# A recurrence and mixture-of-experts kernel: two-block numerator loads, separate natural K and Q, and late Squares without a tie

## The chip, the cores and the metric

The kernel runs on one core of one Trainium2 chip. The metric is the device time of one execution in microseconds, the median of several. Its engines here are TensorE (PE), VectorE (DVE), ScalarE (ACT), GpSimd (POOL) and SyncE (SP), which issues most DMAs.

## The reference

A complex diagonal recurrence with an attention-like read-out (B=4, H=8, S=768, D=48), and behind it a top-1 mixture of experts over the 3072 tokens of width 384:

```python
mag = np.sqrt(a_re * a_re + a_im * a_im)
scale = np.minimum(mag, 0.999) / (mag + 1e-06)
a_re_n, a_im_n = (a_re * scale, a_im * scale)
for t in range(S):
    ar, ai = (a_re_n[:, :, t, :, None], a_im_n[:, :, t, :, None])
    new_re = ar * S_re - ai * S_im
    new_im = ar * S_im + ai * S_re
    kv = np.einsum('bhd,bhe->bhde', k[:, :, t], v[:, :, t])
    S_re, S_im = (new_re + kv, new_im)
    y[:, :, t] = np.einsum('bhd,bhde->bhe', q[:, :, t], S_re)
...
do_compute = x @ w_skip > 0
e_idx = np.argmax(xc @ w_gate, axis=1)
h = np.maximum(xc[mask] @ w1[e], 0.0)
y[mask] = gate_w[mask, None] * (h @ w2[e])
out[do_compute] = xc + y
```

Here x is y with the heads side by side, xc its rows with do_compute, E = 8 experts, F = 1024, and gate_w the chosen expert's softmax weight.

## The kernel before, in words

**Chain and blocks.** The sequence is cut into six chunks c of 128 positions, and pairs of chunks into three groups g. Each chunk is walked from its middle to both ends, so that 64 steps serve 2 sides of 2 chunks for all 32 batch-heads at once (128 partitions). The 64 steps of a group are eight blocks of 8 positions, 24 blocks i in all. For a block, `gate` turns the decay (tile `ain`, four DMAs, L233) into a normalised one: ACT squares (Square, `sq`, L264), DVE adds (L269), ACT takes Ln and Exp (L270, L271, tile `t`), DVE combines (L273), ACT takes Exp (L274), DVE multiplies `ain` by `t` (L360), and ACT writes a negated part (L364). `chain` then runs the running product, two DVE instructions a step (X at L414, W at L423); it waits for nothing but `ain`. `consume` turns the products into weights: ACT squares W (`ws`, L483), PE sums pairs (`sw`, L497), ACT takes Ln and Exp (L505, L506), DVE forms the inverse (L508, L510, L513), and then the numerator rows times W (`nw`, L488, one half K and one half Q) and the denominator rows times inverse (`iw`, L516). PE transposes both (`tp`, L631) and ACT copies them to `qk` (L638). POOL also spills the natural rows to DRAM (`kq`, L544).

**Loads of rows.** `load_qk` loads the tiles `num` (K on the left side, Q on the right) and `inv` (the reverse) for each block: four DMAs each, two a side, from SP.

**Units.** A unit (c,b) is one chunk of one batch. `unit_at` computes the scores pa on PE (L701) and masks them on DVE (`at`, L724); `unit` scales the state (RX, L739), sums it on PE (ps, L750/L751), lets ACT copy it (`st`, L753), adds K·V (ps, L760, from the natural K), lets ACT copy the new state (`T`, L767), multiplies out py (L771, L774), and makes the router logits and rows (yT L778, px L786, lg L797, xa L801), which go out by a DMA (L808). Natural K comes back from `kq` in the tile `nat`: `nat` (L555/L558) is called two units ahead. For the middle group the transposed K and Q are not held: its units' `nat` holds K and Q together (768 KB, L555) and PE transposes both (`tu`, L570). The first two units of that group get theirs in another way: `ahead` loads most of their rows early into `pre` tiles (POOL, L582), `turn_ahead` transposes them (`ta`, L594) and `straight` adds the rest (`ts`, L610).

**Order.** A class `Order` plays a virtual clock while the program is emitted: it picks steps by priority and due time and so fixes in which order instructions reach each engine's in-order queue; the scheduler of the framework refines it by its own model. `issue_after(x)` keeps an instruction from being placed ahead of x. The Square of a gate is held by two such ties, to the last Exp of the gate before (`exp_ins`) and to the last Exp of a consume (`wx_ins`).

After the last unit come the routes, and then the experts one after another (`moe`: tokens L1117 to L1161, ph L1193, hh and hl L1195/L1196, po L1225 to L1227).

Of the kernel before, what the change touches and what calls it, by code (L numbers as in the profile page):

```python
# [20 lines left out]
DM = H * D  # L21
# [92 lines left out]
class Kern:  # L114
# [133 lines left out]
    def load_qk(self, i, name):  # L248
        g, p = divmod(i, NP)
        t = self.ld.tile([128, LP, D], F32, name=f"{name}_{i}", tag=name)  # L250
        left, right = (self.k3, self.q3) if name == "num" else (self.q3, self.k3)
        self.load(g, t, left, 0, p * LP, LP, 0)
        self.load(g, t, right, 1, p * LP, LP, 0)
        return t

    def scale(self, i, n, ain):


        V, A, o = self.nc.vector, self.nc.scalar, self.order
# [8 lines left out]
        with self.tc.issue_after(self.cins) if self.cpos else ExitStack():  # L268
            V.tensor_tensor(u, sq[:, 0], sq[:, 1], ALU.add)  # L269
        A.activation(l, u, AF.Ln, bias=self.tinym)  # L270
        self.t_ins = A.activation(t, l, AF.Exp, scale=-0.5, bias=self.lnw, accum_out=self.acc[:, 1, i:i + 1]).ins  # L271
        yield o.wait(vt(N), o.act(2 * N, 3, o.t + vt(N)))
# [273 lines left out]

    def nat(self, c, b):

        if c == NCH - 1:
            return  # L550
# [3 lines left out]
        if self.spilled(g) and (c, b) not in self.near:  # L554
            self.nc.sync.dma_start(t.rearrange("p h q d -> p (h q) d"),  # L555
                                   self.kq[g][r:r + H].rearrange("h q s d -> s (h q) d"))
        else:
            self.nc.sync.dma_start(t[:, :, 0], self.kq[g][r:r + H, 0].rearrange("h s d -> s h d"))  # L558

    def turn(self, c, b):  # L560

        nc = self.nc
        t = self.nats[c, b]
        qk = self.un.tile([96, H, 4, HC], F32, name=f"qkT_{c}_{b}", tag="qkT")
        for hh in range(2):
            hs = slice(hh * 4, hh * 4 + 4)
            for q in range(2):
                tp = self.ps_tp.tile([96, 4, 2, HC], F32, name=f"tu_{c}_{b}_{hh}_{q}", tag="tp")
                for h in range(4):
                    nc.tensor.transpose(tp[:, h].rearrange("p k t -> p (k t)"), t[:, hh * 4 + h, q], self.ident)  # L570
                o = qk[:, hs, 2 * q:2 * q + 2]
                nc.scalar.copy(o[:, :, :, ::-1] if q else o, tp)
# [3 lines left out]
    def ahead(self, g):  # L576

        nc, n = self.nc, C - 2 * ENDS
        for b in range(NEAR):
            self.pre[b] = self.un.tile([C, H, 2, 2 * D], F32, name=f"pre_{b}", tag="nat")  # L580
            self.near[2 * g, b] = self.un.tile([96, H, 4, HC], F32, name=f"qkT_{2 * g}_{b}", tag="qkT")
            nc.gpsimd.dma_start(self.pre[b][0:n].rearrange("p h q d -> p (h q) d"),  # L582
                                self.kq[g][b * H:b * H + H, :, ENDS:C - ENDS].rearrange("h q s d -> s (h q) d"))

    def turn_ahead(self, c, b):
# [124 lines left out]
    def unit(self, c, b):  # L710
# [44 lines left out]
        if c < NCH - 1:  # L755
            kt = self.nats.pop((c, b))[:, :, 0]
            if ps is None:
# [40 lines left out]
        if c == NCH - 1:  # L798
            hi = self.parts[0][:, b]
            A.copy(hi.rearrange("p (a k) -> p a k", k=2 * D), px[:, :, 0:2 * D])  # L800
# [31 lines left out]
    def rows(self, c):  # L832
# [3 lines left out]
        if c == NCH - 1:  # L836
            self.lg = self.rt.tile([128, B, E + 1], F32, name=f"lg_{c}", tag="lg5")
            self.parts = [self.un.tile([128, B, DM], F32R, name=f"xa{k}", tag="nat") for k in "hl"]
        elif c % 2 == 0:
# [3 lines left out]
    def units(self, g):  # L843
        self.nat(2 * g, 0)
        self.nat(2 * g, 1)
        self.unit_at(2 * g, 0)
# [122 lines left out]
    def route1(self, b):  # L969
# [27 lines left out]
        pt = self.order.pe(200)  # L997
        hi, lo = [t[:, b] for t in self.parts]
        V.tensor_tensor(lo, self.xa[c][:, b, 0:DM], hi, ALU.subtract)
# [51 lines left out]
    def attention(self):  # L1051
        with ExitStack() as ctx:
# [15 lines left out]
            self.pr_ins, self.py_ins, self.T2, self.ain, self.QK, self.Ew, self.T, self.pa, self.W, self.ready, self.nats, self.kqt = [{} for _ in range(12)]  # L1068
            self.F_done = self.cpos = self.gates_done = self.cons_done = self.routes_done = self.units_done = self.v_done = 0
# [60 lines left out]
    def tokens(self, e, xg, xp, pt_, ph_):  # L1130
# [22 lines left out]
        for i, (b, x) in enumerate(((0, self.py_ins[2]), (1, px), (2, px), (-1, pr[3]), (3, pr[3]))):  # L1153
            with self.tc.issue_after(x):
                for k, pt in enumerate(pts):
# [292 lines left out]
```

## Time and profile before

| | us |
|---|---|
| median of 3 runs | 504.09 (503.89 to 505.27) |
| the profiled execution's own time | 504.79 |
| its span in the profile | 503.1 |
| PE busy / DVE busy / ACT busy in the span | 421.0 / 401.8 / 303.2 |
| POOL busy | 99.5 |

The profiled execution is one of its own, 0.70 us above the median. The clock granted to TensorE was 0.902 of full on the mean. Shares of busy time are averages over a first part and a second part with different limits, so the stages are read one by one below. An idle time is printed in brackets with the instruction that ended it.

### The profile page before, as it was taken

How to read it: one execution, taken by the hardware profiler on the slowest of the kernel's cores; microseconds unless marked ns; L12 is line 12 of the kernel's file. 1: busy time of each engine (PE TensorE's matmuls, PEld its weight loads, DVE VectorE, ACT ScalarE, POOL GpSimd, SP SyncE). 2: the span in 40 equal slices, each digit the busy share in tenths (PEclk: the TensorE clock that was granted, in tenths of full speed). 3: DMA queues.
4: the chain of work that ended last, by engine and by line, in shares of the span. 5: the costliest groups of instructions: out<-in, count | busy, mean ns of one | idle time of the engine just before them, and what ended most of it. 6: DMA issues, size and time to landing. Idle time of an engine off the chain costs nothing. (4 is left out here: it accounts for less than half of the span.)

```text
span 503.1 us, 10049 instructions
## 1 busy us (share of the span) xinstructions
PE 421.0 (84%) x3294; PEld 369.7 (73%) x3294; DVE 401.8 (80%) x1009; ACT 303.2 (60%) x702; POOL 99.5 (20%) x171
## 2 busy tenths in 40 slices
PE   0355654499998678889999999998999999999992
PEld 0143432389786567778878889997999999999992
DVE  4999999998989979998897967878788766866630
ACT  5868698656466687568879763332656553755420
POOL 4011111110212412072000020343301211121011
PEclk9966666579999865999999999999999999999997
DMA  4556877688977986587765529775798667865301
GB/s 97 117 120 161 203 169 177 159 205 216 262 177 198 217 207 162 129 205 185 168 173 119 124 56 273 201 208 156 228 295 264 201 203 246 246 195 182 106 23 27
DMA packets 141953, 88.83 MB, mean 177 GB/s; under 512 B 112347, under 2 KB 135372, under 8 KB 141895
## 3 DMA queue, kind: packets, MB, share of 16 engines
q1 hardware_dynamic: 135031, 71.30, 55.3%
q0 software_dynamic: 6224, 16.63, 11.6%
q8 instruction: 28, 0.46, 0.4%
q10 hardware_dynamic: 640, 0.20, 0.2%
q14 instruction: 30, 0.25, 0.2%
HBM read 63.39 MB, written 26.58 MB: 179 GB/s over the span
## 5 line engine op out<-in xcount | busy, mean ns | idle before, releaser
L414 DVE TENSOR_TENSOR X<-W,ain 128x192 f32<-128x192 f32 x192 | 67.7, 353 | 5.6 <-ACT ain L364 2.3
L1118 DVE TENSOR_TENSOR l<-r,h 128x768 fp32r<-128x768 f32 (+1 forms) x53 | 56.6, 1074 | 12.6 <-ACT h L1117 12.5
L497 PE MATMUL sw<-ws,ident 128*128 128x384 f32 x84 | 43.7, 657 | 20.5 <-ACT ws L483 20.3
L1195 ACT ACTIVATE hh<-ph 128x240 fp32r<-128x240 f32 x64 | 23.8, 374 | 52.8 <-PE ph L1193 52.8
L1117 ACT CAST h<-r 128x768 fp32r<-128x768 f32 (+1 forms) x53 | 49.2, 934 | 9.4 <-DMA r<-in_moe_w_dram 9.3
L631 PE MATMUL tp<-ident,iw 128*96 128x128 f32 x128 | 24.7, 347 | 33.1 <-DVE iw L516 29.3
L423 DVE TENSOR_TENSOR W<-X 128x96 f32<-128x96 f32 x192 | 48.7, 254 | 3.5
L1193 PE MATMUL ph<-xh,l 128*128 128x240 f32 x192 | 51.2, 275 | 0.0
L1193 PE MATMUL ph<-xh,h 128*128 128x240 f32 x192 | 49.9, 275 | 0.0
L1193 PE MATMUL ph<-xl,h 128*128 128x240 f32 x192 | 49.5, 276 | 0.2 <-DVE xl L1147 0.2
L631 PEld LDWEIGHTS tp<-ident,iw 128*96 128x96 f32 x128 | 18.8, 162 | 36.4 <-ACT t L271 19.6
L638 ACT COPY qk<-tp 96x256 f32<-96x256 f32 x128 | 39.6, 370 | 6.7 <-PE tp L631 6.3
L1225 PE MATMUL po<-h,hh 128*120 128x384 f32 x128 | 43.4, 339 | 0.0
L497 PEld LDWEIGHTS sw<-ws,ident 128*128 128x128 f32 x84 | 19.2, 250 | 32.6 <-ACT ws L483 22.6
L1226 PE MATMUL po<-l,hh 128*120 128x384 f32 x128 | 42.9, 337 | 0.0
L1227 PE MATMUL po<-h,hl 128*120 128x384 f32 x128 | 41.1, 343 | 0.0
L771 PE MATMUL py<-at,vt 128*64 128x128 f32 x384 | 40.2, 280 | 0.0
L880 POOL DMA_INDIRECT xs<-xa,sl x24 | 28.3, 1180 | 42.5 <-DVE sl L953 22.1
L1193 PEld LDWEIGHTS ph<-xh,l 128*128 128x128 f32 x192 | 36.4, 189 | 0.0
L1196 DVE SCALAR_TENSOR_TENSOR hl<-ph,hh 128x240 fp32r<-128x240 f32 x64 | 25.7, 403 | 13.1 <-ACT hh L1195 13.0
L724 DVE TENSOR_TENSOR at<-pa,mask 128x512 f32<-128x512 f32 x48 | 32.6, 684 | 4.3 <-PE pa L701 4.2
L1193 PEld LDWEIGHTS ph<-xh,h 128*128 128x128 f32 x192 | 35.6, 189 | 0.3 <-issue 0.2
(254 smaller groups left out, 1078.1 us busy)
## 6 DMA issues: line engine op xcount, KB each, us to landing
r<-in_moe_w_dram SPq DMA_DIRECT2D x24, 512.0 KB, 5.1
r<-in_moe_w_dram SPq DMA_DIRECT2D x32, 384.0 KB, 7.5
kq<-nw POOLq DMA_DIRECT2D x24, 192.0 KB, 3.8
kq<-iw POOLq DMA_DIRECT2D x24, 192.0 KB, 3.3
vt<-in_v_dram SPq DMA_DIRECT2D x24, 192.0 KB, 3.4
out_dram<-xa SPq DMA_DIRECT2D x24, 192.0 KB, 2.8
nat<-kq SPq DMA_DIRECT2D x6, 768.0 KB
ain<-in_a_im_dram SPq DMA_DIRECT2D x90, 48.0 KB, 2.7
```

The lines of the kernel that those rows point to most:

```text
L414: V.tensor_tensor(X, prev.unsqueeze(1).to_broadcast([128, 2, 2, D]), windows(ain[:, :, j]), ALU.mult)
L423: self.cins = V.tensor_tensor(W[:, j, ::-1], X[:, :, 0], X[:, :, 1], ALU.add).ins
L497: nc.tensor.matmul(sw, self.ident, ws[:, :, c], start=(c == 0), stop=(c == 1))
L631: nc.tensor.transpose(tp[:, jj], src[:, s * 4 + jj], self.ident)
L638: nc.scalar.copy(o, tp[:, :, :, cc].rearrange("p j s b -> p b s j"))
L771: PE.matmul(py[j * 64:j * 64 + 64, hp], vt_[:, 2 * hp + j], at[:, 2 * hp + j], start=True, stop=(c == 0))
L1117: nc.scalar.copy(hi[:, ks], raw)
L1118: nc.vector.tensor_tensor(lo[:, ks], raw, hi[:, ks], ALU.subtract)
L1193: pe = PE.matmul(ph, w[:, k, js], x[:, k], start=(n == 0), stop=(n == len(terms) - 1))
L1225: PE.matmul(po, hh[:, j, sl], w2h[:, j], start=(j == 0), stop=False)
L1226: PE.matmul(po, hh[:, j, sl], w2l[:, j], start=False, stop=False)
L1227: pe = PE.matmul(po, hl[:, j, sl], w2h[:, j], start=False, stop=(j == NF - 1))
```

## The change

Four edits. (1) `load_qk`: a `num` tile holds 16 rows and is loaded every second block; block i+1 takes its half from a dictionary. `inv` stays at 8 rows. (2) Natural K lies in two tiles that live through the attention part, kn0 and kn1 (units in turn, 384 KB each, for all c under 5); natural Q lies in tiles `natq`, loaded only for the middle group's units other than the first two, at L576 of the changed kernel, two units ahead of its use in `unit_at`. The rows loaded ahead are split likewise: their K goes to kn0 and kn1, their Q to `natq` tiles, four POOL DMAs of half the size instead of two. (3) The Square of `scale` keeps its ties for i under 19 only, and that of `scale_last` loses the tie to `wx_ins`. (4) The tiles for the last chunk's rows in two parts (xah, xal) are cut in two, to fit the new tags. `SUMS` is empty, so the branch on it is never taken, and `LOADED` is not used.

```diff
+SUMS = ()
+TIED = 19
...
     def load_qk(self, i, name):
         g, p = divmod(i, NP)
-        t = self.ld.tile([128, LP, D], F32, name=f"{name}_{i}", tag=name)
-        left, right = (self.k3, self.q3) if name == "num" else (self.q3, self.k3)
-        self.load(g, t, left, 0, p * LP, LP, 0)
-        self.load(g, t, right, 1, p * LP, LP, 0)
-        return t
+        rows = LP * self.rows_at_once[name]
+        ts = self.kqs[name]
+        if i not in ts:
+            t = self.ld.tile([128, rows, D], F32, name=f"{name}_{i}", tag=name)
+            left, right = (self.k3, self.q3) if name == "num" else (self.q3, self.k3)
+            self.load(g, t, left, 0, p * LP, rows, 0)
+            self.load(g, t, right, 1, p * LP, rows, 0)
+            for k in range(rows // LP):
+                ts[i + k] = t[:, k * LP:k * LP + LP]
+        return ts.pop(i)
...
-        with self.tc.issue_after(self.exp_ins), self.tc.issue_after(self.wx_ins):
+        with self.tc.issue_after(self.exp_ins), self.tc.issue_after(self.wx_ins) if i < TIED else ExitStack():
             A.activation(sq, ain[:, 0:2], AF.Square, scale=1.0 / 0.999)
...
-        with self.tc.issue_after(self.exp_ins), self.tc.issue_after(self.wx_ins):
+        with self.tc.issue_after(self.exp_ins):
             A.activation(sq, ain[:, 0:2], AF.Square, accum_out=self.acc[:, 0, i:i + 1])
...
-    def nat(self, c, b):
+    def knat(self, n):
+        return self.kns[n % 2]
+
+    def nat(self, n, end):
+        while self.k_done <= n and self.k_done < min(end, (NCH - 1) * B):
+            self.nc.sync.dma_start(self.knat(self.k_done), self.rows_of(*divmod(self.k_done, B), 0))
+            self.k_done += 1
+
+    def natq(self, c, b):
+        if self.spilled(c // 2) and (c, b) not in self.near:
+            t = self.natqs[c, b] = self.half(f"natq_{c}_{b}")
+            self.nc.sync.dma_start(t, self.rows_of(c, b, 1))
...
-        t = self.nats[c, b] = self.un.tile([C, H, 2, 2 * D], F32, name=f"nat_{c}_{b}", tag="nat")
...
     def turn(self, c, b):
-        t = self.nats[c, b]
+        t = self.knat(c * B + b), self.natqs.pop((c, b))
...
-            self.pre[b] = self.un.tile([C, H, 2, 2 * D], F32, name=f"pre_{b}", tag="nat")
+            self.pre[b] = self.knat(2 * g * B + b), self.half(f"pre_{b}")
...
-            nc.gpsimd.dma_start(self.pre[b][0:n].rearrange("p h q d -> p (h q) d"),
-                                self.kq[g][b * H:b * H + H, :, ENDS:C - ENDS].rearrange("h q s d -> s (h q) d"))
+            for q in range(2):
+                nc.gpsimd.dma_start(self.pre[b][q][0:n], self.rows_of(2 * g, b, q, ENDS, C - ENDS))
...
+            nx = c * B + b + 2
+            if (c, b) not in self.near and nx < (c // 2 + 1) * 2 * B:
+                self.natq(*divmod(nx, B))
...
-        nx = c * B + b + 2
-        if nx < (c // 2 + 1) * 2 * B:
-            self.nat(*divmod(nx, B))
+        nx = c * B + b + 3
+        if b == 0 and c % 2 == 0:
+            self.natq(*divmod(nx, B))
+        self.nat(nx - 1, (c // 2 + 1) * 2 * B)
...
+            self.kns = [self.half(f"kn{i}", "nat") for i in range(2)]
...
+            self.kqs, self.rows_at_once = dict(num={}, inv={}), dict(num=2, inv=1)
```

Because the planner's costs and the tiles change, the order of other instructions moves too. Lines of the changed kernel are higher by 2 to 34; the names say which instruction it is. On ACT, at the block 19's gate and unit (2,0)'s state, the order before was (sq and t are block 19's, st, ps and T unit (2,0)'s, ws block 17's):

```order
L270 ACTIVATE sq_2275<-sq_2275,col 128x384
L271 ACTIVATE t_2276,acc<-sq_2275,col 128x384
L274 ACTIVATE t_2276,acc<-sq_2275 128x384
L753 COPY st_165<-ps_0_2355 96x8x48
L767 COPY T_0_2367<-ps_0_2355 96x384
L364 ACTIVATE ain_2198<-ain_2198 128x384
L483 ACTIVATE ws_2530<-W_2327 128x768
```

and in the changed kernel (qk from tp is the copy of block 16's transposed iw, the second Square, on `ain_2222`, is block 20's):

```order
L285 ACTIVATE sq_2231<-sq_2231,col 128x384
L784 COPY st_165<-ps_0_2306 96x8x48
L286 ACTIVATE t_2232,acc<-sq_2231,col 128x384
L666 COPY qk_0_2136<-tp_0_2_2458 96x32x2x4
L666 COPY qk_1_2137<-tp_0_2_2458 96x32x2x4
L666 COPY qk_0_2136<-tp_1_2_2465 96x32x2x4
L666 COPY qk_1_2137<-tp_1_2_2465 96x32x2x4
L289 ACTIVATE t_2232,acc<-sq_2231 128x384
L272 ACTIVATE sq_2675<-ain_2222 128x768
L798 COPY T_0_2318<-ps_0_2306 96x384
```

The copy st moved ahead of both Exps of block 19, the four copies of block 16's transposed iw came ahead of the second Exp, and block 20's Square, 31 rows further down before, now stands right behind it.

On SP, around the loads of natural rows for the middle group's units, before (num and inv are block 18's, nat_2 is unit (2,2)'s 768 KB, ain block 21's):

```order
L233 DMA num_2456<-in_k_dram 32x8x48 x2
L233 DMA num_2456<-in_q_dram 32x384 x2
L233 DMA inv_2522<-in_q_dram 32x8x48 x2
L233 DMA inv_2522<-in_k_dram 32x384 x2
L555 DMA nat_2_2563<-kq_119 128x16x96
L233 DMA ain_2713<-in_a_re_dram 32x8x48
L686 DMA vt_170<-in_v_dram 128x8x48
L233 DMA ain_2713<-in_a_re_dram 32x8x48
```

and in the changed kernel (kn_171 and kn_172 are kn0 and kn1, first for units (2,0) and (2,1), at the end kn0 for (2,2); ain_2222 is block 20's and ain_2666 block 21's; inv is block 18's; natq_2 and natq_3 are the Q halves of (2,2) and (2,3)):

```order
L569 DMA kn_171<-kq_119 128x8x96
L569 DMA kn_172<-kq_119 128x8x96
L236 DMA ain_2222<-in_a_re_dram 32x8x48 x2
L236 DMA ain_2222<-in_a_re_dram 32x384 x2
L236 DMA ain_2222<-in_a_im_dram 32x8x48 x2
L236 DMA ain_2222<-in_a_im_dram 32x384 x2
L576 DMA natq_2_2240<-kq_119 128x8x96
L576 DMA natq_3_2514<-kq_119 128x8x96
L236 DMA inv_2473<-in_q_dram 32x8x48 x2
L236 DMA inv_2473<-in_k_dram 32x384 x2
L236 DMA ain_2666<-in_a_re_dram 32x8x48
L569 DMA kn_171<-kq_119 128x8x96
```

Unit (2,2)'s Q half moved ahead of block 18's inv, its K half stands behind it and behind the first DMA of block 21's ain. Block 18's num has gone from here: it was loaded with two blocks together earlier.

On DVE, from block 19's gate sum to block 16's iw, before (the last row is iw of block 16; X and W are block 17's steps; sq is block 19's; oh, cnt, ohs and cand are the router's):

```order
L269 TENSOR_TENSOR sq_2275<-sq_2275 128x384
L414 TENSOR_TENSOR X_5_2425<-W_2327,ain_2041 128x192
L508 TENSOR_TENSOR ws_2303<-sw_2417,ws_2303 128x8x48
L423 TENSOR_TENSOR W_2327<-X_5_2425 128x2x48
L510 SCALAR_TENSOR_TENSOR ws_2303<-ws_2303 128x8x48
L414 TENSOR_TENSOR X_6_2440<-W_2327,ain_2041 128x192
L273 SCALAR_TENSOR_TENSOR sq_2275<-sq_2275,t_2276 128x384
L513 SCALAR_TENSOR_TENSOR inv_2218<-inv_2218,ws_2303 128x384
L423 TENSOR_TENSOR W_2327<-X_6_2440 128x2x48
L965 TENSOR_TENSOR ohs<-ohs,cnt_2503 128x8
L944 TENSOR_TENSOR cand_2395<-oh_2397,pr_2430 128x64
L516 TENSOR_TENSOR iw_2505<-inv_2218,W_2189 128x768
```

and in the changed kernel up to the same iw:

```order
L973 RECIPROCAL xa_1499<-se_2342 128x4
L957 TENSOR_TENSOR oh_2348<-oh_2348,act_2341 128x64
L976 SCALAR_TENSOR_TENSOR base_2343<-act_2341,base_2343 128x8
L523 TENSOR_TENSOR ws_2259<-sw_2368,ws_2259 128x8x48
L438 TENSOR_TENSOR W_2278<-X_3_2357 128x2x48
L997 TENSOR_REDUCE cnt_2454<-oh_2348 128x8
L525 SCALAR_TENSOR_TENSOR ws_2259<-ws_2259 128x8x48
L429 TENSOR_TENSOR X_4_2363<-W_2278,ain_2002 128x192
L528 SCALAR_TENSOR_TENSOR inv_2174<-inv_2174,ws_2259 128x384
L438 TENSOR_TENSOR W_2278<-X_4_2363 128x2x48
L284 TENSOR_TENSOR sq_2231<-sq_2231 128x384
L531 TENSOR_TENSOR iw_2456<-inv_2174,W_2145 128x768
```

iw and the ws and inv ahead of it moved up past two X steps, block 19's sum stands just ahead of iw, and block 19's second step (sq from t) comes behind it. A few rows further on, block 17's ws (L508) stands ahead of the masking at of unit (2,1) (L724); before, it stood behind it. Near 165 to 180 us two more swaps: PE has the first ta of unit (2,0) ahead of sw_14, and DVE the gate product ain_16 ahead of ws_14. Behind 198 us PE has sw_16 ahead of the transposes of nw_16.

## Rows read from the trace of the kernel before

**Rows 1.** Stages (us; us, then per engine busy (instructions); PEclk, DMA share, GB/s)
```profile
165.00:200.00 35.00, 25.60 (x154) 22.08 (x153) 31.53 (x85) 26.52 (x67) 10.20 (x19) 0.65 0.84 195
200.00:205.00 5.00, 5.00 (x27) 4.45 (x27) 4.95 (x21) 1.50 (x6) 0.08 (x1) 0.73 0.82 185
...
205.00:210.50 5.50, 3.70 (x32) 2.62 (x30) 5.50 (x26) 3.35 (x8) 0.00 (x0) 1.00 0.48 119
...
220.00:260.00 40.00, 39.37 (x339) 32.51 (x338) 33.57 (x79) 31.87 (x77) 9.32 (x12) 1.00 0.75 182
...
400.00:495.00 95.00, 93.85 (x686) 93.51 (x685) 58.54 (x97) 43.81 (x84) 15.05 (x16) 1.00 0.55 169
```

**Rows 2.** The longest waits of PE from 226 to 495 us (in all, times, longest)
```profile
PE px L786 <- ACT yT L778: 1.5, 3, 0.6
```

**Rows 3.** PE in order of time (start us, us, instruction, [idle before <-releaser])
```profile
176.04 2.91 PE L497 MATMUL sw<-ws,ident 128*128 128x384 f32 x4
...
198.74 3.78 PE L701 MATMUL pa<-qkT 96*128 96x128 f32 x16 [0.56 <-ACT qkT L616]
...
207.68 0.81 PE L751 MATMUL ps<-RX,perm 96*96 96x384 f32 x2
...
210.52 1.56 PE L760 MATMUL ps<-vt,nat 128*96 128x48 f32 x16 [1.81 <-ACT st L753]
...
213.70 1.08 PE L631 MATMUL tp<-ident,iw 128*96 128x128 f32 x8
214.61 1.46 PE L497 MATMUL sw<-ws,ident 128*128 128x384 f32 x4
...
219.64 1.05 PE L570 MATMUL tu<-ident,nat 128*96 128x128 f32 x8 [1.46 <-DMA nat<-kq]
```

**Rows 4.** ACT in order of time, same columns
```profile
199.01 0.85 ACT L483 ACTIVATE ws<-W 128x768 f32<-128x768 f32 x1
...
209.49 0.52 ACT L274 ACTIVATE t<-sq 128x384 f32<-128x384 f32 x1 [0.75 <-DVE sq L273]
...
210.01 0.46 ACT L753 COPY st<-ps 96x384 f32<-96x384 f32 x1
```

**Rows 5.** SP in order of time, and DMA issues with KB and us to landing
```profile
211.20 0.82 SPq L233 DMA_DIRECT2D inv<-in_q_dram  x2
...
213.51 0.38 SPq L555 DMA_DIRECT2D nat<-kq  x1
213.99 2.37 SPq L233 DMA_DIRECT2D ain<-in_a_re_dram  x1
...
nat<-kq SPq DMA_DIRECT2D x10, 384.0 KB, 3.9
```

**Rows 6.** DVE in order of time from 206 us
```profile
206.22 0.32 DVE L414 TENSOR_TENSOR X<-W,ain 128x192 f32<-128x192 f32 x1
...
207.54 0.55 DVE L508 TENSOR_TENSOR ws<-sw,ws 128x384 f32<-128x384 f32 x1
```

**Rows 7.** The numerator's loads: one, the tile's view, and the first user on DVE
```profile
12.00 0.91 SPq L233 DMA_DIRECT2D num<-in_q_dram  x2
...
DMA to landing us min/median/max: 2.0/3.0/4.1
...
17.82 0.95 DVE L488 TENSOR_TENSOR nw<-num,W 128x768 f32<-128x768 f32 x1
```

**Rows 8.** Waits of DVE from 222 to 300 us, same columns
```profile
DVE ain L360 <- ACT t L274: 2.5, 2, 1.5
DVE X L414 <- ACT ain L364: 2.3, 2, 1.7
```

**Rows 9.** DVE near 179 us, and POOL's loads ahead of it
```profile
177.97 0.56 DVE L273 SCALAR_TENSOR_TENSOR sq<-sq,t 128x384 f32<-128x384 f32 x1 [0.74 <-ACT t L271]
...
180.33 0.56 DVE L508 TENSOR_TENSOR ws<-sw,ws 128x384 f32<-128x384 f32 x1 [0.84 <-ACT ws L506]
...
167.26 1.84 POOL L582 DMA_DIRECT2D pre<-kq  x2 [0.54 <-issue]
```

More of the change, by code (lines that the diff above doesn't have):

```diff
@@ L41 @@
 VX = 12
+SUMS = ()
+TIED = 19
+LOADED = 1500
 NEAR, ENDS = 2, 3 * LP
@@ L267, in scale @@
         yield o.wait(0, o.act(2 * N, 1, o.t + (2500 if i else 6000)))
-        with self.tc.issue_after(self.cins) if self.cpos else ExitStack():
-            V.tensor_tensor(u, sq[:, 0], sq[:, 1], ALU.add)
-        A.activation(l, u, AF.Ln, bias=self.tinym)
+        m2, cost, done = u, vt(N), o.t + vt(N)
+        if i in SUMS:
+            m2 = self.ps_at.tile([128, n, D], F32, name=f"m2_{i}", tag="pa")
+            for c in range(2):
+                self.nc.tensor.matmul(m2, self.ident, sq[:, c], start=(c == 0), stop=(c == 1))
+            cost, done = 0.0, o.pe(2600)
+        else:
+            with self.tc.issue_after(self.cins) if self.cpos else ExitStack():
+                V.tensor_tensor(u, sq[:, 0], sq[:, 1], ALU.add)
+        A.activation(l, m2, AF.Ln, bias=self.tinym)
         self.t_ins = A.activation(t, l, AF.Exp, scale=-0.5, bias=self.lnw, accum_out=self.acc[:, 1, i:i + 1]).ins
-        yield o.wait(vt(N), o.act(2 * N, 3, o.t + vt(N)))
+        yield o.wait(cost, o.act(2 * N, 3, done))
         V.scalar_tensor_tensor(u, l, 0.0, t, ALU.max, ALU.add)
@@ L545, in keep, with half, rows_of @@
                                      src[side * 64:side * 64 + m].rearrange("p j c d -> p j (c d)"))
-    def nat(self, c, b):
-        if c == NCH - 1:
-            return
+    def knat(self, n):
[8 more added lines that the diff above has]
+            self.nc.sync.dma_start(t, self.rows_of(c, b, 1))
+    def half(self, name, tag="natq", pool=None):
+        return (pool or self.un).tile([C, H, 2 * D], F32, name=name, tag=tag)
+    def rows_of(self, c, b, q, t0=0, t1=C):
         g, cc = divmod(c, 2)
-        t = self.nats[c, b] = self.un.tile([C, H, 2, 2 * D], F32, name=f"nat_{c}_{b}", tag="nat")
         r = cc * BH + b * H
[L554 to L558, printed above, removed]
+        return self.kq[g][r:r + H, q, t0:t1].rearrange("h s d -> s h d")
     def turn(self, c, b):
         nc = self.nc
-        t = self.nats[c, b]
+        t = self.knat(c * B + b), self.natqs.pop((c, b))
         qk = self.un.tile([96, H, 4, HC], F32, name=f"qkT_{c}_{b}", tag="qkT")
@@ L755, in unit @@
         if c < NCH - 1:
-            kt = self.nats.pop((c, b))[:, :, 0]
+            kt = self.knat(c * B + b)
             if ps is None:
@@ L798, in unit @@
         if c == NCH - 1:
-            hi = self.parts[0][:, b]
+            hi = self.parts[0][b // 2][:, b % 2]
             A.copy(hi.rearrange("p (a k) -> p a k", k=2 * D), px[:, :, 0:2 * D])
@@ L837, in rows @@
             self.lg = self.rt.tile([128, B, E + 1], F32, name=f"lg_{c}", tag="lg5")
-            self.parts = [self.un.tile([128, B, DM], F32R, name=f"xa{k}", tag="nat") for k in "hl"]
+            self.parts = [[self.un.tile([128, 2, DM], F32R, name=f"xa{k}{j}", tag=t) for j in range(B // 2)]
+                          for k, t in (("h", "natq"), ("l", "nat"))]
         elif c % 2 == 0:
@@ L843, in units @@
     def units(self, g):
-        self.nat(2 * g, 0)
-        self.nat(2 * g, 1)
+        n, end = 2 * g * B, (2 * g + 2) * B
+        self.nat(n + 1, end)
+        self.natq(2 * g, 2)
         self.unit_at(2 * g, 0)
@@ L997, in route1 @@
         pt = self.order.pe(200)
-        hi, lo = [t[:, b] for t in self.parts]
+        hi, lo = [t[b // 2][:, b % 2] for t in self.parts]
         V.tensor_tensor(lo, self.xa[c][:, b, 0:DM], hi, ALU.subtract)
@@ L1067, in attention @@
             self.scat, self.pre, self.near, self.xa = [], {}, {}, {}
-            self.pr_ins, self.py_ins, self.T2, self.ain, self.QK, self.Ew, self.T, self.pa, self.W, self.ready, self.nats, self.kqt = [{} for _ in range(12)]
-            self.F_done = self.cpos = self.gates_done = self.cons_done = self.routes_done = self.units_done = self.v_done = 0
+            self.pr_ins, self.py_ins, self.T2, self.ain, self.QK, self.Ew, self.T, self.pa, self.W, self.ready, self.natqs, self.kqt = [{} for _ in range(12)]
+            self.F_done = self.cpos = self.gates_done = self.cons_done = self.routes_done = self.units_done = self.v_done = self.k_done = 0
             self.rx_t = 0.0
             self.cq, self.routes = [], []
+            self.kqs, self.rows_at_once = dict(num={}, inv={}), dict(num=2, inv=1)
             o = self.order = Order()
@@ L1160, in tokens @@
                     for n, xa in enumerate(self.parts):
-                        PE.matmul(pt, xa[:, b, ks(k)], self.ohx[b], start=(i + n == 0), stop=True, skip_group_check=True)
+                        PE.matmul(pt, xa[b // 2][:, b % 2, ks(k)], self.ohx[b], start=(i + n == 0), stop=True, skip_group_check=True)
         A.copy(xh[:, 0], pts[0])
```

4 lines of the change are left out of this document (2 added, 2 removed).

## The prediction, as it was made

> **What bounds the kernel now.** I read the table of stages first [rows 1]. Ahead of 220 us DVE carries the program: 31.53 of 35 us busy from 165 to 200, 5.50 of 5.50 from 205 to 210.5. From 220 us on PE is full: 39.37 of 40 at once, 93.85 of 95 in the last long stretch. So the end is the moment at which PE becomes full, near 219.6 us, plus a fixed pile of PE work. A change counts if it moves that moment, or opens or closes a gap in PE behind it. The gaps behind it are small: from 226 to 495 us the largest group of waits is 1.5 us in all [rows 2].
>
> The waits just ahead of that moment come next [rows 3]. PE waits 1.81 us at 210.52 for ACT's copy st (L753) before unit (2,0)'s K·V product, and 1.46 us at 219.64 for the transfer of `nat` before the transposes tu (L570) of unit (2,2). Behind them stand two causes. ACT's copy st starts at 210.01 although PE wrote its input by 208.5 (L751 at 207.68, 0.81 long): t_19's two Exps (L271, L274) stand ahead of it in ACT's order, the second after a wait of 0.75 for DVE [rows 4]. And the 768 KB of `nat` are issued only at 213.51, behind inv_18's loads, which waited for iw_16 (L516) until 211.20 [rows 5]; PE could start 6.1 us after the issue.
>
> **The change, part by part.** The sum is made against the profiled execution's own 504.79 us; the median of the three runs is 504.09, so I carry the difference over to the median. About 0.3% (1.5 us) is what a measurement here can tell from no change.
>
> *Numerator rows for two blocks.* 48 of the 96 DMAs of 48 KB go, and the other 48 double: two of them held SP 0.91 us [rows 7], so 22 us of SP's time in all, and as many bytes move as before. No engine's waits behind 20 us name `num` [rows 2, 3, 8], so this is worth 0. What covers its risk: the first load is twice as long, and its user (nw, L488) starts at 17.82 us, while the load was issued from 12.00 to 12.91 [rows 7] and a load of this kind lands 2.0 to 4.1 us after issue [rows 7], thus by 17.0 at the latest; twice the bytes cost at most a few tenths more than that. Cover 0.8 us; if it breaks, DVE loses those tenths at the start and so does the end.
>
> *Natural K and Q apart.* The bytes are the same; unit (2,2)'s Q half is issued ahead of inv_18's loads (second order fence), its K half behind them and behind the first ain_21 load, and not before unit (2,0)'s K·V product has read kn0, which ends about 212.1. A 384 KB load landed 3.9 us after issue [rows 5], against 6.1 for 768 KB. On DVE ws_16 (L508) and with it iw_16 stand ahead of five instructions more (X and W of the chain, cnt, sq_19's sum; third order fence), which from 206.22 to ws_16's start at 207.54 hold 1.3 us [rows 6], and with the W behind them some 1.5: iw_16 ends near 209.6 instead of 211.1. So inv_18's loads, which take some 2.2 us before the next issue (211.20 to 213.51 [rows 5]), end near 211.8; K is issued at 212.3, or, if the ain_21 load ahead of it takes SP the 2.37 us that one took at 213.99, at 214.3. It lands between 216.2 and 218.2. PE reaches tu, walking its new order with the durations of [rows 3], near 217.2. So of the 1.46 us between 0.5 and 1.46 go; I take 1.2, nearer the early issue, since the long ain load stood behind 768 KB just issued. The Trainium skill speaks against splitting: "DMA: Bandwidth & Descriptors", section Bandwidth, asks for transfers of 1 MiB and more, since each pays a fixed cost. The trace bears that out (6.1 us for 768 KB, 3.9 for half), and if the halves came one behind the other, 7.8 us would stand against 6.1 and the 1.2 would go.
>
> *The order near 208 to 220.* st is now ahead of t_19's Exps (first order fence), and PE has iw_16's transposes (1.08 us for eight, at 213.70 [rows 3]) ahead of the K·V product, in the gap of 1.81. They can run from 209.7 to 210.7, so the K·V product starts 0.2 later than now with 1.1 us of work less behind it: 0.9, which I take; the whole 1.81 is the upper bound, 0 the lower, if DVE's iw_16 is no earlier than it was. On the other side DVE gets ws_17 (L508) ahead of unit (2,1)'s masking `at` in its order; ws_17 needs sw_17, which by the same walk comes through ACT's Ln and Exp near 217.7, so DVE idles about 1 us there. PE waits for it only at py of (2,1) and RX of (2,1), where it is 1 to 2 us ahead, so I take 0, at worst -1.0.
>
> *The stretch 165 to 200.* ta of unit (2,0) goes ahead of sw_14, its copy ahead of sq_16's Ln, which starts some 0.4 us later (a copy such as st takes 0.46 [rows 4]); DVE waited 0.74 for that chain at 177.97 and 0.84 for ws_14 at 180.33 [rows 9]. Now ain_16 stands ahead of ws_14; by the same durations DVE waits about 1.1 and 0.8, 1.9 for 1.6. That is -0.3 on an engine that sets the end. The K half of the rows loaded ahead is the first of four smaller transfers from 167.26 on [rows 9], and its transposes run behind sw_14, which ended near 179: 11 us of cover, where a load of 768 KB landed within 6.1.
>
> *Squares no longer tied (i of 19 and up).* They free DVE of waits for ACT behind 222 us: 2.5 for t (L274) and 2.3 for ain (L364) [rows 8]. PE is full there, so this is worth 0 in the time; its use is slack for DVE, which repays the 1 us above. If PE were not full, up to 4.8 us.
>
> *The rest.* The MoE part has the same order; the split of the parts xa hi/lo changes no instruction. 0.
>
> Sum: 0.9 + 1.2 - 0.3 = 1.8 us less: 503.0 for the profiled execution, **502.3 us** against the median.
>
> **Rivals.**
> 1. *Nothing arrives* (504.1). DVE is never idle from 205 to 210.5 [rows 1]; if the 1 us of idle at ws_17 and the later RX hold PE back where it would be ahead, or K lands at 218.2 or later, both gains end as other waits. For: two engines are near their limit at once. Against: iw_16 itself moves forward on DVE.
> 2. *Slower: PE's clock comes up later.* The granted clock was 0.65 from 165 to 200, 0.73 from 200 to 205 and 1.00 after [rows 1]; sw's pair took 2.91 us at the lower level (176.04) and 1.46 at the full one (214.61) [rows 3]. It rose while PE worked without a gap behind 198.74. The new order puts sw_16 ahead of nw_16's transposes there, and sw_16 needs ACT's ws_16. If that opens a gap of a microsecond and the half clock stays until 210, the 3.70 us of work that PE did between 205 and 210.5 [rows 1] takes 3.7 more; 1.8 of that falls into the old gap, and with rival 1 the time is 504.1 + 1.9 = 506.0. It decides at sw_16: no gap, no rival. Against: ACT writes ws_16 from 199.01 to 199.86 [rows 4], while pa keeps PE busy until 202.5 [rows 3]. "TensorE: Matmul & The Clock Gate" of the Trainium skill, Part 1, says that the low clock is the default and steady work releases it; by that rule, a gap there would cost in this way, and the trace agrees (0.65 in a stretch with PE busy 25.60 of 35).
> 3. *More is won* (500.3): the 1.81 and 1.46 go whole, the -0.3 stays, and the waits behind 226 halve with the new places of the ACT copies: 504.1 - 3.3 - 0.8 + 0.3. For: those waits are for an ACT copy [rows 2].
> 4. *The change does not do what it says*: the Squares are freed, but sit in ACT's order ahead of copies that PE needs; a Square of this width takes 0.85 us (ws at 199.01 [rows 4]), four of them (sq_20 to sq_23) make at worst 3.4 us of PE gaps; half of that with nothing won gives 504.1 + 1.7 = 505.8. Against: ACT is busy only 31.87 of 40 us there [rows 1].
>
> **How the numbers follow.** The forecast, a gain of 1.0 to 2.6 us, has 0.42; rival 3 has 0.10; rival 1 has 0.28; rivals 2 and 4 have 0.11 and 0.09. The forecast's lower part (under 1.5 us) counts as no change: 0.04 of it. So faster by over 0.3% (under 502.6) 0.48, within 0.3% 0.32 (0.28 + 0.04), slower (over 505.6) 0.20. The range reaches from a little below rival 3's time, 500.0, to rival 2's, 506.0, and leaves out less than half of each, some 0.04 and 0.1. The forecast's own range is 501.5 to 503.1.
>
> **What would show it.** Right: iw_16's transposes run before the K·V product of (2,0), st copied before 209.5, tu of (2,2) starting before 218.5 with a wait under 0.5 us, PE becoming full 1.5 to 2.5 us earlier, and the stretch behind it unchanged in PE work; DVE waits at ain and X behind 222 gone without moving the end. Wrong: K landing behind 218.5, a wait for RX or `at` of (2,1) on PE of over 1 us, the clock at its lower level behind 205, ACT Squares ahead of a copy that PE waits for, or DVE later at 198 by more than 0.5 us.

## The result, and the profile after

The changed kernel takes **498.98 us** (median of 4 runs, 497.84 to 499.60); the kernel before took 504.68 on the same chip (503.89 to 506.97). The ratio is 0.9875, interval 0.9841 to 0.9909: faster by 1.2%, or 6.3 us by the ratio. The forecast was 1.8 us; the time lies below the low end of the range. The profiled execution took 499.22 us with a span of 497.5; before it was 504.79 and 503.1. So 5.6 us are to be found between the two traces.

The table of stages of the changed kernel, against [rows 1] (us; us, then per engine busy (instructions) in the order PE, PEld, DVE, ACT, POOL; PEclk, DMA share, GB/s):

```profile
165.00:200.00 35.00, 27.65 (x157) 24.16 (x157) 33.25 (x92) 25.70 (x66) 11.38 (x21) 0.64 0.81 194
...
205.00:210.50 5.50, 5.50 (x58) 4.35 (x58) 5.45 (x21) 3.96 (x12) 1.15 (x2) 1.00 0.81 194
220.00:260.00 40.00, 39.84 (x361) 32.78 (x360) 36.59 (x87) 33.62 (x85) 6.46 (x11) 1.00 0.69 174
```

DVE does 33.25 us of work from 165 to 200 where it did 31.53, and from 205 to 210.5 PE is full where it was busy 3.70 of 5.50.

To find where the 5.6 us arise I cut both programs at the same piece of work: the transposes tpe at the end of block 15, which follow directly on those of iw_15 (ts). Before they started at 197.54, after at 195.14. **2.4 us are won ahead of that point.** Behind it, the same columns, first the kernel before:

```profile
197.54:222.00 24.46, 20.39 (x158) 16.84 (x158) 24.02 (x84) 14.36 (x37) 7.14 (x9) 0.89 0.71 167
222.00:345.00 123.00, 121.90 (x1179) 104.82 (x1179) 100.31 (x274) 77.21 (x192) 26.48 (x32) 1.00 0.65 166
345.00:493.80 148.80, 147.65 (x1123) 145.51 (x1119) 101.00 (x212) 73.73 (x140) 25.70 (x28) 1.00 0.63 194
```

And the changed kernel:

```profile
195.14:222.00 26.86, 26.61 (x191) 21.01 (x191) 26.00 (x89) 16.93 (x45) 11.11 (x10) 0.87 0.84 206
222.00:345.00 123.00, 121.78 (x1218) 105.76 (x1217) 102.97 (x290) 74.96 (x188) 22.26 (x32) 1.00 0.60 159
345.00:488.30 143.30, 142.39 (x1048) 140.75 (x1048) 96.43 (x192) 71.64 (x135) 24.86 (x27) 1.00 0.62 195
```

PE is practically full from 195 us on, where it became full near 219.6 before. Its idle time up to 222 us falls from 24.46 - 20.39 = 4.07 to 0.25; from there to 345 it is 1.10 and 1.22, and up to PE's last matmul 1.15 and 0.91. Together **3.9 us less idle**. Against it stand some 0.8 us, because more of the work now falls on the lower clock (0.87 of 26.86 us, 0.89 of 24.46). 2.4 + 3.9 - 0.8 = 5.5, of 5.6.

The second part is what the prediction spoke of. PE in the changed kernel (start us, us, instruction, [idle before <-releaser]), against [rows 3]:

```profile
195.14 0.64 PE L677 MATMUL tpe<-ident,e 128*96 128x128 f32 x2
...
207.47 1.05 PE L659 MATMUL tp<-ident,iw 128*96 128x128 f32 x8
208.36 1.48 PE L791 MATMUL ps<-vt,kn 128*96 128x48 f32 x16
...
214.85 0.60 PE L598 MATMUL tu<-ident,kn 128*96 128x128 f32 x4
```

iw_16's transposes stand ahead of the K·V product, and the waits of 1.81 for st and 1.46 for `nat` are both gone. ACT's copy st and SP's loads (same columns) show why, against [rows 4, 5]:

```profile
207.01 0.45 ACT L784 COPY st<-ps 96x384 f32<-96x384 f32 x1
```

```profile
207.35 0.84 SPq L236 DMA_DIRECT2D inv<-in_q_dram  x2
...
210.02 0.40 SPq L569 DMA_DIRECT2D kn<-kq  x1
```

st is copied at 207.01, not 210.01. inv_18's loads go at 207.35, not 211.20, and unit (2,2)'s K half at 210.02, 4.8 us ahead of its transposes.

The first part, 2.4 us ahead of 197.5, the prediction did not have at all: it expected 0.3 us of loss there. DVE carries that part: up to tpe it is busy 175.8 us before and 175.6 after, and its waits from 20 us on are 8.1 us in all before and 5.7 after: the 2.4 us. Before (in all, times, longest):

```profile
DVE ws L508 <- ACT ws L506: 3.2, 5, 0.8
DVE sq L273 <- ACT t L271: 2.6, 7, 0.7
...
DVE nw L488 <- PE ts_True L610: 0.6, 1, 0.6
```

and after:

```profile
DVE ws L523 <- ACT ws L521: 3.1, 6, 0.8
DVE sq L288 <- ACT t L286: 1.1, 5, 0.3
```

From 165 us on they are 2.3 before (the 0.74 and 0.84 of [rows 9] and the 0.6 for nw) and 0.5 after. The experiments are about this part first.

### The profile page after: what moved, and what is told of

It is laid out like the page before. It is cut to its first block, busy times and chain, and to the rows that moved or that the text cites. A ratio compares the mean times of both kernels' runs of the same rounds, so it can differ in the third digit from the quotient of the medians.

```text
span 497.5 us, 10005 instructions
## 1 busy us (share of the span) xinstructions
PE 419.4 (84%) x3294; PEld 368.3 (74%) x3294; DVE 401.6 (81%) x1009; ACT 301.6 (61%) x702; POOL 99.5 (20%) x173
## 5 line engine op out<-in xcount | busy, mean ns | idle before, releaser
L1267 POOL DMA_INDIRECT out_dram<-og,idx x16 | 19.7, 1228 | 83.2 <-DVE og L1266 46.2
L914 POOL DMA_INDIRECT xs<-xa,sl x24 | 26.9, 1121 | 45.5 <-DVE sl L987 20.2
```

## The experiments

The expectations set two theories of the gain against each other, beside others. **SP's time** (Theory B): SP issues loads without a gap for long stretches, and a load that gates need is late because SP was busy with others; 48 DMAs fewer give that time back. **The order** (Theory A): the time comes from where the instructions now stand on each engine, whichever edit moved them. Every kernel's time is told as a ratio to the kernel before on the same chip, since that kernel itself took 504 to 507 us on some chips and 518 on another. The traces are of one execution each.

### One part alone

The two-block numerator loads, put into the kernel before (`load_qk` as in the change, and this line):

```diff
+ self.kqs, self.rows_at_once = dict(num={}, inv={}), dict(num=2, inv=1)
```

> Theory A (order: each part gains where it moves the order of instructions): the two-block numerator loads alone change DVE's order from block 12 on, at about 150 us, so they give the part of the gain between 150 and 198 us: 1.0 to 1.6 us less than before, nothing between 100 and 115 us. Theory B (queue: fewer DMAs on SP make every load land earlier): this part alone gives most of the 5.6 us, 3 to 5 us less. As predicted blind: 0.

Measured: 499.6 us, ratio **0.9881** (0.9826 to 0.9937). Nearly the whole gain, from the part that the sum put at 0. tpe starts at 194.97, as in the changed kernel, and DVE's waits up to it are 5.4 us. Of the two of [rows 9] 0.18 is left at sq and nothing at ws (DVE, start us, us, instruction):

```profile
176.63 0.56 DVE L278 SCALAR_TENSOR_TENSOR sq<-sq,t 128x384 f32<-128x384 f32 x1 [0.18 <-ACT t L276]
...
178.25 0.96 DVE L365 TENSOR_TENSOR ain<-ain,t 128x768 f32<-128x768 f32 x1
...
179.29 0.55 DVE L513 TENSOR_TENSOR ws<-sw,ws 128x384 f32<-128x384 f32 x1
```

The gate's product ain stands ahead of the weights ws here, so DVE has work while ACT makes them; near 158 and 168 us ws stands first. In the kernel before all three pairs stand reversed (ain 158.19, ws 159.23; ain 169.20, ws 170.44; ws 180.33, ain 180.97). With them iw_13 starts at 170.37, not 172.45, and PE's transposes of it at 171.37, not 173.46. In the kernel before ACT waited 1.42 us, until 176.26, to copy the outcome of these transposes (qkT), and block 16's Ln and Exp stood behind that copy; in num_alone it waits for DVE's sum ahead of them, 0.64 us. The changed kernel has the same three pairs as num_alone. No load need come earlier for this: ACT's Squares wait 4.6 us for DMAs from 60 to 230 us in num_alone and 4.4 before. The other 2.9 us of num_alone arise behind tpe and are not broken down here.

K and Q in tiles of their own alone (the change with `dict(num=1, inv=1)` and all Squares tied):

> Theory A: natural K and Q apart change PE's order from about 100 us on and remove the wait for nat at 219.6, so they give 0.9 us between 100 and 115 us and 1.5 to 2 us between 198 and 222: 2.0 to 3.0 us less than before. Theory B: little, under 1 us, since as many bytes and more DMAs go through SP.

Measured: 504.67 us, ratio **0.9979** (0.9945 to 1.0013): no change that shows.

The freed Squares alone:

```diff
- with self.tc.issue_after(self.exp_ins), self.tc.issue_after(self.wx_ins):
+ with self.tc.issue_after(self.exp_ins), self.tc.issue_after(self.wx_ins) if i < TIED else ExitStack():
```

> Theory A: the untied Squares change DVE's order from 222 us on only, where PE is full, so 0 to 0.9 us less than before; DVE's waits for ACT's t and ain behind 222 us, 4.8 us in all, go. Rival C (PE is not really full behind 222 us and follows DVE): 2 to 4 us less.

Measured: 509.22 us, ratio **1.0057** (1.0014 to 1.0101): slower. Two things lie in its profile. Behind 222 us rival 4 is there as described: a Square stands directly ahead of the copy st, and PE waits. ACT, then PE:

```profile
238.30 0.83 ACT L265 ACTIVATE sq<-ain 128x768 f32<-128x768 f32 x1
239.03 0.46 ACT L754 COPY st<-ps 96x384 f32<-96x384 f32 x1
```

```profile
239.54 1.56 PE L761 MATMUL ps<-vt,nat 128*96 128x48 f32 x16 [0.74 <-ACT st L754]
```

The other lies ahead of 222, where this kernel has the same order of instructions as the one before. The Square of one gate there, in this kernel and in the kernel before:

```profile
201.59 0.84 ACT L265 ACTIVATE sq<-ain 128x768 f32<-128x768 f32 x1 [3.41 <-DMA inv<-in_k_dram]
```

```profile
196.54 0.84 ACT L264 ACTIVATE sq<-ain 128x768 f32<-128x768 f32 x1 [0.27 <-DMA inv<-in_k_dram]
```

The same instruction waits 3.41 us for a DMA in one execution and 0.27 in the other. Everything behind it on ACT is late by that: the copies qkT, for which PE waits 3.71 us at 203.79 before the products pa (0.56 in [rows 3]). In 23 executions of the kernel before on that chip the time ran from 503.40 to 512.11 us; how long this wait was in them no trace shows. The row names `inv`, but what the Square reads is `ain`. SP in the kernel before shows where that load stands (start us, us, instruction):

```profile
186.06 1.01 SPq L233 DMA_DIRECT2D num<-in_k_dram  x2
187.11 1.44 SPq L233 DMA_DIRECT2D num<-in_q_dram  x2
188.65 0.86 SPq L233 DMA_DIRECT2D inv<-in_q_dram  x2
189.55 0.45 SPq L233 DMA_DIRECT2D inv<-in_k_dram  x1
190.11 1.80 SPq L233 DMA_DIRECT2D ain<-in_a_re_dram  x4
191.96 2.54 SPq L233 DMA_DIRECT2D ain<-in_a_im_dram  x4
194.53 0.42 SPq L233 DMA_DIRECT2D inv<-in_k_dram  x1
```

Each row follows the last within 0.3 us, from 179.5 on and up to 206.93, and SP's waits in that time are 3.0 us in all, so `ain` goes out when SP reaches it. A DMA of 48 KB takes 0.45 us of SP, four of `ain` 1.80; `num` takes some 2.4 us ahead of them here. The last of `ain` was issued by 194.50, the page gives `ain` 2.7 us from issue to landing, and the Square started at 196.54: no slack. In num_alone SP stands still from 202.52 to 208.83, before from 206.93 to 211.20.

In ties_alone, though, the load was not late because SP was busy with others. SP stood still from 173.16 to 178.32, by the trace for a DMA (`inv`, 5.1 us), and worked without a gap from there on:

```profile
171.11 2.05 SPq L234 DMA_DIRECT2D ain<-in_a_re_dram  x4
178.32 2.21 SPq L234 DMA_DIRECT2D ain<-in_a_im_dram  x4
...
195.76 2.04 SPq L234 DMA_DIRECT2D ain<-in_a_im_dram  x4
```

The last `ain` of that Square went out by 197.80, 3.3 us later than before. With its queue full SP did not make up for the stop. The kernel before has such a stop too, 3.9 us near 174 for `ain`, with the DMA engines busy all the while (share 1.05 to 1.16 from 172 to 178).

### Is it the number of DMAs?

The two-block tile, but filled by eight DMAs of 48 KB, as many as before. First in the kernel before:

```diff
- self.load(g, t, left, 0, p * LP, rows, 0)
+ for k in range(rows // LP):
+     self.load(g, ts[i + k], left, 0, (p + k) * LP, LP, 0)
```

(and the same for `right`; an excerpt).

> The kernel before, with the numerator's rows loaded for two blocks at once, but in eight DMAs of 48 KB instead of four of 96 KB: as many DMAs on SP as before, 96. Theory B (SP's issue time, 0.45 us for each DMA, makes the loads of ain late near 196 us): no gain, within 1.5 us of before, and ACT's Square of block 19 waits for a load. Theory A (the order that two-block loads bring): the gain of num_alone stays, 4 us or more.

Measured: 519.77 us, ratio **1.0047** (0.9998 to 1.0096), against 0.9881 with four larger DMAs. The same edit in the changed kernel:

> The changed kernel with its two-block numerator rows brought by eight DMAs of 48 KB instead of four of 96 KB, nothing else changed. Theory B (SP's issue time): the gain goes, within 0.5% of before. If the number of DMAs on SP mattered only for the kernel before, the gain of 1.2 to 1.4% stays.

Measured: 507.78 us, ratio **1.0013** (0.9979 to 1.0047), against 0.9859 for the changed kernel in another set (below). The bytes and the tiles are the same, the DMAs are twice as many, and the gain is gone in both. But the number of DMAs is not all that differs. DVE's order is back as well: the three pairs of ain and ws stand as in the kernel before. And the eight DMAs stand in one row ahead of `ain`, some 5 us of SP where four take some 2 before. In num_two_blocks_small SP, and ACT's Square that follows:

```profile
80.22 1.98 SPq L233 DMA_DIRECT2D num<-in_k_dram  x2
82.24 1.20 SPq L233 DMA_DIRECT2D num<-in_q_dram  x2
83.48 0.92 SPq L233 DMA_DIRECT2D num<-in_k_dram  x2
84.44 0.91 SPq L233 DMA_DIRECT2D num<-in_q_dram  x2
```

```profile
91.16 0.84 ACT L269 ACTIVATE sq<-ain 128x768 f32<-128x768 f32 x1 [2.49 <-DMA ain<-in_a_im_dram]
```

The kernel before has this Square at 86.00 without a wait. So here the queue does make a load late; but block 19's Square, whose wait was expected, ran at 201.33 without one. The waits of ACT's Squares for DMAs from 60 to 230 us (in all, times, longest), in the kernel before:

```profile
ACT sq L264 <- DMA num<-in_k_dram: 2.5, 1, 2.5
...
ACT sq L264 <- DMA ain<-in_a_im_dram: 1.6, 2, 1.2
...
ACT sq L264 <- DMA inv<-in_k_dram: 0.3, 1, 0.3
```

in the kernel before with the eight small DMAs:

```profile
ACT sq L269 <- DMA ain<-in_a_im_dram: 8.0, 4, 2.5
...
ACT sq L269 <- DMA inv<-in_q_dram: 4.5, 2, 3.3
```

in the changed kernel with them:

```profile
ACT sq L272 <- DMA ain<-in_a_im_dram: 10.4, 4, 5.0
...
ACT sq L272 <- DMA num<-in_k_dram: 2.5, 1, 2.5
...
ACT sq L272 <- DMA inv<-in_q_dram: 1.7, 1, 1.7
```

and in the changed kernel:

```profile
ACT sq L272 <- DMA ain<-in_a_im_dram: 3.7, 2, 2.1
```

4.4, 12.5, 14.6 and 3.7 us. tpe starts at 197.54, 201.96, 204.15 and 195.14. These waits go some way to tell the loss with the small ones, but not the gain (4.4 against 3.7). DVE's waits up to tpe tell both: 8.1, 13.2, 14.6 and 5.7 us, and tpe's start less these is 189.4, 188.8, 189.6 and 189.4. num_two_blocks_small ran on the chip where the kernel before took 518 us; no_num (below), on the same chip with as many DMAs but block by block, has tpe at 196.97. So these two runs show what eight DMAs in a row cost; they do not show that the gain is SP's time and not the order.

### Other ways to relieve SP

The kernel before with the numerator's right-hand loads issued on POOL:

```diff
- self.load(g, t, right, 1, p * LP, LP, 0)
+ self.load(g, t, right, 1, p * LP, LP, 0, self.nc.gpsimd if name == "num" else None)
```

> The kernel before, with the numerator's right-hand loads (48 of 48 KB) issued by POOL instead of SP, block by block as before. Theory B: SP is rid of 48 DMAs as in the change, so 3 to 6 us less than before, and the Square of block 19 waits for no load. Theory A: within 1.5 us of before, or slower, since POOL's spills come later.

Measured: 513.67 us, ratio **0.9894** (0.9826 to 0.9962; 4 runs). The DMAs are still small and as many; SP no longer issues 48 of them. DVE keeps the order of the kernel before, and tpe starts at 196.88, beside 196.97 in no_num on the same chip: ahead of tpe nothing is won. No trace of the kernel before on that chip shows where the 1.1% arise.

The kernel before with the denominator's rows (`inv`) in two-block loads instead of the numerator's, `dict(num=1, inv=2)`:

> The kernel before, with the denominator's rows (inv) loaded for two blocks at once in place of the numerator's: 48 DMAs fewer on SP as well, but another order. Theory B: 3 to 6 us less than before. Theory A: some other time, no reason for the same gain; 0 to 2 us less.

Measured: 511.11 us, ratio **0.984** (0.9759 to 0.9921; 4 runs). So a gain of this size is not special to the numerator. The 2.4 us ahead of tpe are, as far as the traces show: here tpe starts at 197.14, with DVE's pairs as in the kernel before.

The changed kernel with `dict(num=1, inv=2)`:

> The changed kernel with the denominator's rows loaded for two blocks at once in place of the numerator's: as many DMAs on SP as the change has, another order. Theory B: within 0.4% of the changed kernel, 0.982 to 0.992 of before.

Measured: 506.68 us, ratio **0.9982** (0.9952 to 1.0011): a miss. As many DMAs are saved, and nothing comes of it. PE there waits 2.2 us for the masking `at`, 2.8 for st and 1.4 for `kn`, groups that are 0.5, 0.7 and absent in the changed kernel. tpe starts at 197.65, with DVE's pairs as in the kernel before. No kernel gained 1% without fewer DMAs on SP, but fewer DMAs are not sufficient: with each edit the planner also writes another order, and that moves the time by 1% too.

The changed kernel with the denominator's right-hand loads on POOL besides:

> The changed kernel with the denominator's right-hand loads (48 of 48 KB) issued by POOL. Theory B with SP still the limit: 1 to 4 us faster than the changed kernel. Theory B with SP no longer the limit after the change: within 1 us, or slower by what POOL's own issues delay (its scatters and spills).

Measured: 501.12 us, ratio **0.9906** (0.9878 to 0.9935); nothing more is won, and by the medians of the ratios 0.5% is lost, though the intervals still touch. As far as this run shows, SP's time no longer sets that kernel's end.

### The change without one part

Without the two-block loads (`dict(num=1, inv=1)`):

> The changed kernel with the numerator's rows loaded block by block again (K and Q apart, Squares free). Theory B: the gain is gone, 500 to 507 us with a scatter as wide as that of before (some 9 us between runs). Theory A as far as the first runs bear on it: the same, as the two parts left gave -0.2% and +0.6% alone.

Measured: 518.02 us, ratio **0.9961** (0.992 to 1.0003). What the prediction costed, the split, the order and the freed Squares, is worth 0.4% together, 2 us, with an interval that reaches 1; the prediction had 1.8.

Without the freed Squares (all tied again), in two sets, the second beside the unedited changed kernel:

> The changed kernel with the Squares tied again, the other two parts kept. Theory A: 0 to 0.9 us above the changed kernel, so 4.7 to 5.6 us less than before. Rival C: 2 to 4 us above the changed kernel, 1.6 to 3.6 us less than before.

> The changed kernel with the Squares tied again. If freeing the Squares is worth 0, as predicted, it is within 1 us of the changed kernel on the same chip; if their freedom costs, as it did alone (+0.6%), it is 1 to 3 us faster than the changed kernel.

> The changed kernel itself, as the yardstick for the next three on the same chip: 0.980 to 0.992 of before.

Measured: 499.99 us, ratio 0.9896 (0.9842 to 0.995), and 500.05, ratio **0.9875** (0.9847 to 0.9903), beside 499.18, ratio **0.9859** (0.9828 to 0.9889). Freeing the Squares is worth at most some 0.9 us here and may be worth nothing. Ties up to another block (`TIED = 21`, `TIED = 12`):

> The changed kernel with the ties kept for the first 21 gates instead of 19. If the freed Squares are worth 0 as predicted: within 0.3% of the changed kernel. If freeing early matters: between no_ties_again and changed_again, whose medians differ by 0.9 us.

> The changed kernel with the ties kept for the first 12 gates only, so that Squares from block 12 on, in the stretch that DVE and the loads bound, stand behind the Exp of the gate before. If a Square that is placed early stands in ACT's queue waiting for its load: 2 to 6 us slower than the changed kernel. If it only gives slack: within 1.5 us.

Measured: 500.74 us, ratio 0.987 (0.9829 to 0.9912), and 501.4, ratio 0.9881 (0.984 to 0.9922): 19 is as good as any of them.

Without the split (natural K and Q in one tile, two-block loads and freed Squares kept):

> The changed kernel with natural K and Q in one tile again (two-block numerator, Squares free). If the blind term holds (1.2 us for the late K half, 0.9 for the order), it is about 2 us slower than the changed kernel; PE waits again for nat before the transposes of unit (2,2), 1 to 3 us. If the split is worth nothing once SP is relieved, as num_alone against no_ties says (499.6 and 500.0), it is within 1 us.

Measured: 506.07 us, ratio **0.9988** (0.9959 to 1.0017). Here the split carries 1.3%, though alone it showed nothing and num_alone does without it. The profile shows a wait that can account for it. PE in order of time, then the granted clock around it (columns as in the table of stages):

```profile
303.32 1.53 PE L766 MATMUL ps<-vt,nat 128*96 128x48 f32 x16 [1.70 <-DMA nat<-kql]
```

```profile
302.00:305.00 3.00, 1.68 (x19) 1.71 (x20) 2.59 (x9) 0.00 (x0) 0.00 (x0) 1.00 1.00 350
305.00:308.00 3.00, 3.00 (x18) 2.44 (x17) 1.48 (x4) 0.26 (x1) 0.00 (x0) 0.56 0.96 323
308.00:311.00 3.00, 3.00 (x20) 3.00 (x20) 2.20 (x9) 0.00 (x0) 0.00 (x0) 0.50 0.22 70
311.00:314.00 3.00, 3.00 (x20) 2.77 (x21) 0.70 (x7) 0.00 (x0) 0.00 (x0) 0.50 0.49 124
314.00:317.00 3.00, 3.00 (x33) 2.82 (x30) 0.69 (x1) 0.87 (x2) 0.00 (x0) 0.74 0.06 15
```

PE waits 1.70 us for `nat` and is busy 1.68 of 3 us; then the granted clock is at the lower of its two levels, 1.2 GHz, for three windows with PE busy throughout. Worked out: 0.44 + 0.50 + 0.50 + 0.26 of 3 us each are 5.1 us of PE work lost, and with the wait 6.8. The loss is (0.9988 - 0.9859) x 505.6 = 6.5 us. This is one profile, of an execution that took 509.08, in a kernel whose runs went from 502.26 to 513.50, so not every run need have this wait; in this one PE also waits 2.3 us for `at` and 2.0 for `nat` elsewhere. The changed kernel's profile has neither the wait nor the fall of the clock. no_split also has 48 DMAs fewer on SP, DVE's pairs as in num_alone and an early tpe (195.70), and yet no gain: what is won ahead of tpe is lost behind it.

## Why the prediction was wrong

- **Numerator rows for two blocks: "worth 0".** This step failed. Its reason was that no engine's waits behind 20 us name `num`. That does not hold: ACT's Square at 98.35 waited 2.5 us for a DMA of that name (first line of the Squares' waits above), and [rows 2, 3, 8] show PE and DVE only. But this wait was not the gain either; in num_alone it is 2.2. The step priced the loads and left out that the edit also moves DVE's order. Measured: the part alone gives 0.9881, 6 us, and without it the change shows 0.9961. In place of the 0 the traces show 2.4 to 2.6 us ahead of tpe, as DVE's waits fall from 8.1 to 5.7 and 5.4 with the new order; why the rest comes with this part stays open.
- **The stretch 165 to 200: "-0.3".** Wrong in sign: of the 2.4 us, 1.8 arise from 165 on. The two waits of [rows 9] were to grow from 1.6 to 1.9; in the changed kernel they are 0.17 ahead of sq, none ahead of ws and 0.35 ahead of ain, and the 0.6 for nw is gone. The prediction had the swap of ain and ws near 180, but not those near 158 and 168, with which iw_13, PE's transposes of it and block 16's Ln come earlier.
- **Natural K and Q apart: 1.2.** The mechanism was right: K went out at 210.02, 2.3 us ahead of the earliest time given, and the whole wait of 1.46 [rows 3] is gone. Its size depends on what is beside it: nothing that shows alone, 1.3% beside two-block loads and freed Squares, where in the one profile a wait took the clock with it. So splitting transfers did no harm here, while the edit that merges 48 KB into 96 KB for the numerator was the larger gain. The rule of the Trainium skill that was weighed there ("DMA: Bandwidth & Descriptors", section Bandwidth) asks for larger transfers. These runs do not show that it is the reason: from 165 to 200 us the DMAs moved 195 GB/s before [rows 1] and 194 after.
- **The order near 208 to 220: 0.9.** Right in its steps (iw_16 first, st at 207.01, no wait at tu). It sits in the fall of PE's idle time from 4.07 to 0.25, of which 3.27 are the two waits named. With the 1.2 above it was put at 2.1; measured are 3.8 less idle, some 0.8 of it paid back to the lower clock.
- **Freed Squares: 0.** Right beside the other two parts. Alone it is slower by 0.6%. Rival 4's mechanism is real (the wait of 0.74 at 239.54); the changed kernel's trace has no wait for st behind 222.
- **Rivals.** Rival 3, more is won, was the nearest, for half of its reasons: the 1.81 and 1.46 went whole, but PE's idle time behind 222 did not halve (2.25 and 2.13 us), and the stretch ahead of 200 it left at -0.3. That it came nearest is luck in part: 2.4 of the 5.6 us arose where it had a loss. Rival 2's gap at sw_16 did not come: it ran at 199.40 without a wait, and the clock was 1.00 from 205 on.

What is open. The numerator's 6 us are shown by adding the part and by taking it away; how they come about is shown in part only. Ahead of tpe the traces speak for the order. With num_alone's three pairs tpe starts at 194.6 to 195.7 (seven traces, one more at 197.10, of that kernel's slowest run); with those of the kernel before at 196.1 or later (nine traces), and three of these have 48 DMAs fewer on SP; tied_12 has a mixture, and 198.19. But no kernel has the new order without the relief of SP, so the order alone is not tested. For SP's time speak the two other ways to save issues, which gained 1.1 and 1.6% in four runs each; against it as a sufficient cause speak changed_inv_two and no_split, which save as many and gain nothing. That the transfers themselves are what SP and the Squares wait for, as in ties_alone, is a third reading that no run separates. A version with both `num` and `inv` in two-block loads was not tried.

## What to carry to other kernels

Where a planner writes the order, an edit whose own price is 0 can still move the engine that sets the stage. Add up that engine's waits in both traces first: here the difference of DVE's, 8.1 against 5.7 us, was the time won ahead of tpe, while the waits at the place that the edit was thought to relieve hardly changed. And test a cause with a run that keeps the order: a variant that takes the cause away and brings the old order back decides nothing.

Look at the issuing queue as an engine, too: each DMA of 48 KB held SP 0.45 us, and eight in a row ahead of `ain` made a Square wait 2.49 us that had not waited. One profile says little of such a wait: at the same instruction it was 0.27 us in one trace and 3.41 in another.

## What was not expected of the hardware

The issue of a load took SP 0.91 us for two DMAs of 48 KB [rows 7], 1.02 us for two of `kn` at 384 KB in the changed kernel, and 0.38 for one of 768 KB [rows 5]: the time in the queue hardly follows the size. And a wait of PE has two prices. After the 1.46 us of [rows 3], with PE busy 1.54 of the 3 us from 217 to 220, the clock was 1.00 from 220 to 260 [rows 1]: the wait cost its length. In no_split a wait of 1.70, in a 3 us stretch in which PE was busy 1.68, was followed by 9 us at 0.50 to 0.56 and cost four times its length. In num_alone PE was busy 0.58 of the 3 us from 214 to 217, with a wait of 2.70 for `nat`, and the granted clock was 0.65 and 0.78 in the next two stretches of 3 us. What decides between the two prices these rows do not show.
